# Two constants made on other engines, one table load first, and a planner told when engines begin

## The chip, the cores and the metric

The kernel runs on one core of one Trainium2 chip. The core has a matrix engine (PE, with a queue of weight loads, PEld), a vector engine (DVE), a scalar engine with function tables (ACT), Pool and SyncE (SP), which here only starts transfers. All engines run their own instruction queue in order and meet through semaphores. The metric is the device time of one execution in microseconds (us), and a time is the median over several runs.

## The reference

Linear attention without a softmax is followed by a two-layer network with softplus. The bridge between them turns (batch, head, row, feature) into 4608 tokens of 512 features.

```python
kv  = einsum('bhsd,bhse->bhde', k, v)          # 8 batches, 8 heads, 576 rows, 64 features
o   = einsum('bhsd,bhde->bhse', q, kv)
o   = o / sqrt(mean(o*o, -1) + 1e-6) * g_norm  # g_norm: 64 numbers
x   = o, heads beside each other               # 4608 x 512
h   = x @ w_in                                 # 512 x 2048
g   = maximum(h, 0) + log1p(exp(-abs(h)))
out = g @ w_out                                # 2048 x 512
```

The inputs q, k, v and g_norm are 32-bit floats. The two weight matrices come in 64-bit floats, and the kernel reads each value as two 32-bit words.

## The kernel before

**Precision by parts.** PE multiplies in a reduced 32-bit format (fp32r), so each operand of the two large products is split into a high part and two low ones. A step of the first product (`mm1`, L668) is 12 matmuls of 384 columns: 3 parts by 4 blocks of 128 features. A step of the second (`mm2`, L675) is 3 groups of 3 matmuls of 512 columns. 16 chunks of 128 hidden features times 12 blocks of 384 tokens make 192 steps, in three phases of chunks, with the partial output written to memory between phases.

**Weights.** Each of 32 pieces (16 chunks of w_in, 16 of w_out, 128 x 512 values) is loaded in 512 KB of raw words (`fetch`, L275) into one of two buffers `raw`. Then ACT makes a square from the upper words (`square`, L286), DVE builds the 32-bit value (`high1` L290, `high2` L294, `mask` L299, which reads ACT's square, `power` L307, `rest` L312, `total` L316), and ACT sums what is beyond range (L303). A raw buffer is free again after `rest`. `divide` makes the three parts: ACT the high part (L348), DVE the remainder (L351), ACT the second part (L355). For the first four chunks the third part comes from PE: two matmuls, one with the identity (L366) and one with the negative identity `minus_r` (L367), whose sum ACT scales (L370).

**Attention.** For each batch, `kv_of` loads k and v (L491, L493, the last 64 rows as `tail` in L483 and L485) and multiplies them on PE (L505 for batches 0 and 1, L513 otherwise and for the tails), and ACT copies the result to `kv_diag` (L520, L521). `rows` does 128 tokens: q is turned (PE L585 and ACT L592 for the first two batches, DVE L560 later), multiplied with kv (L530), squared on ACT (L598), summed on DVE (L535), raised to the power -0.5 on Pool (L538, L539), scaled on DVE (L542), and turned on PE (L547). `split` makes the three parts of x^T with g_norm as a factor by partition: ACT the high part with `g_down` (L437), which is g_norm times a number just under 1, DVE the others with `g_col` (L440, L444). ACT copies x^T for later phases (L607), and SP stores it (L608).

**Order.** Nothing is scheduled by the framework. The kernel adds tasks with an estimated duration, dependencies, buffers and a place in the order (`pos`) to a `Plan`. `Plan.order` (L67) plays the tasks through on five engines and one transfer server: it keeps a date at which each engine and the transfers are free, takes the task that can begin first (among those within `SOON` = 150 ns on one engine, the lowest `pos`), and gives it its buffers. The dates are only used for the order in which each engine gets its instructions; on the chip everything runs as its waits allow. A transfer may be issued when its server will be free within 2500 ns, and lands 2000 ns after its own share of the server. While PE has nothing planned before the first `mm1`, the plan puts filler matmuls of the identity in (`warm`, L784), from `BEGIN` = 4000 ns on, as many of 400 ns as fit before the next real task.

**The preamble.** Before the planned tasks, L747 to L758 issue by hand: two small loads of g_norm into `g_col` from ACT's queue (L748), `g_down` on ACT (L749), the table of softplus for ACT (L750), the identity on Pool (by a helper), its fp32r copy on DVE (L753), `minus_r` on ACT (L754), and memsets on DVE (L755 to L758). The table that holds softplus also serves ACT's other functions in this kernel: after L750 the trace has no other table load.

Of the kernel before, what the change touches and what calls it, by code (L numbers as in the profile page):

```python
# [13 lines left out]
ALU = mybir.AluOpType  # L14
# [8 lines left out]
DOWN_G = 1.0 - 0.99 * 2.0 ** -13  # L23
# [17 lines left out]
class Plan:  # L41
# [2 lines left out]


    HANDOVER = {"PE": 250, "ACT": 120, "DVE": 120, "POOL": 150, "SP": 0}
    BEGIN = 4000
    SOON = 150

# [17 lines left out]
    def order(self):  # L67
        waiting = {id(t): len(t.after) + (t.follows is not None) for t in self.tasks}
        users = {}
        for t in self.tasks:  # L70
            for a in t.after + ([t.follows] if t.follows else []):
                users.setdefault(id(a), []).append(t)
        ready = {}
        for t in self.tasks:
            if not waiting[id(t)]:
                t.ready = 0
                ready.setdefault(t.engine, []).append(t)
        free = {r: [(0, i) for i in range(n)] for r, n in self.rings.items()}
        engine_free = {"PE": 0, "ACT": 0, "DVE": 0, "POOL": 0, "SP": 0}
        dma_free = 0  # L80
        last_read = {}
        done, left = [], len(self.tasks)
        while left:
            best = None
            for engine, tasks in ready.items():
                options = []
                for t in tasks:
                    at = max(engine_free[engine], t.ready)
                    if t.size:
                        at = max(at, dma_free - 2500)  # L90
                    for i, s in enumerate(t.take):
                        others = sum(u.ring == s.ring for u in t.take[:i])
                        if len(free[s.ring]) <= others:
                            break
                        at = max(at, sorted(free[s.ring])[others][0])
                    else:
                        options.append((at, t))
                if not options:
                    continue
                first = min(at for at, _ in options)  # L100
                at, t = min(((at, t) for at, t in options if at <= first + self.SOON),
                            key=lambda o: (o[1].pos, o[0]))
                if engine == "PE" and self.spare and self.spare[-1].start is None:
                    ring, run, ns, _ = self.spare
                    begin = max(engine_free["PE"], self.BEGIN, min(free[ring])[0] if free[ring] else at)
                    if begin + ns <= at:
                        s = Slot(ring)
                        at, t = begin, Task("PE", ns, lambda s=s: run(s), [], 0.0, [s], [s], 0)
                        s.readers = 1
                if best is None or at < best[0]:  # L110
                    best = (at, t)
            if best is None:
                raise RuntimeError("the plan is stuck at " + str([(e, t.pos, [s.ring for s in t.take if not free[s.ring]]) for e, ts in ready.items() for t in ts][:20]))
            at, t = best
            if t in ready[t.engine]:
                ready[t.engine].remove(t)
                left -= 1
            for s in t.take:
                place = min(free[s.ring])
                free[s.ring].remove(place)  # L120
                s.place = place[1]
            t.start = at
            engine_free[t.engine] = at + t.ns
            t.end = at + t.ns + self.HANDOVER[t.engine]
            if t.size:
                dma_free = max(dma_free, at + t.ns) + t.size
                t.end = dma_free + 2000
            for s in t.give:
                s.readers -= 1
                last_read[id(s)] = max(last_read.get(id(s), 0), t.end)  # L130
                if not s.readers:
                    free[s.ring].append((last_read[id(s)], s.place))
            for u in users.get(id(t), ()):
                waiting[id(u)] -= 1
                if not waiting[id(u)]:
                    u.ready = max([a.end for a in u.after] + ([u.follows.start] if u.follows else []), default=0)
                    ready.setdefault(u.engine, []).append(u)
            done.append(t)
        return sorted(done, key=lambda t: t.start)
# [3 lines left out]
def kernel(  # L143
# [24 lines left out]
    nc = tc.nc  # L168
# [31 lines left out]
    ident = ident_r.bitcast(F32)  # L200
    minus_r = const.tile([P, P], F32R, name="minus_r")
    g_col = const.tile([P, 1], F32, name="g_col")
    g_down = const.tile([P, 1], F32, name="g_down")
# [542 lines left out]

    for e in range(2):  # L747
        nc.scalar.dma_start(out=g_col[e * D:(e + 1) * D], in_=g_norm.rearrange("(d one) -> d one", one=1))  # L748
    nc.scalar.mul(g_down, g_col, DOWN_G)  # L749
    nc.scalar.preload_act_table_set("softplus")  # L750
    scratch = kv_diag[0][:, 0]
    make_identity(nc, scratch)
    nc.vector.tensor_copy(ident_r, scratch)  # L753
    nc.scalar.mul(minus_r, ident, -1.0)  # L754
    nc.vector.memset(half, -0.5)  # L755
    nc.vector.memset(big, 2.0 ** 30)
    for x in kv_diag + tails:
# [62 lines left out]
```

## Time and profile before

| | |
|---|---|
| median of 6 runs | 918.31 us (917.41 to 919.20) |
| the profiled execution | 919.17 us |
| its span, first to last instruction | 917.4 us |
| mean granted PE clock | 0.992 |
| PE busy | 897.9 us (98%) |
| DVE, ACT, Pool busy | 626.6, 414.7, 80.3 us |
| read from and written to memory | 91.75 and 38.80 MB |
| first `mm1` matmul (L668) | 43.21 us |
| last stretch of matmuls | 909.09 to 913.47 us |

Times within a profile are microseconds from the start of its span. A line of the timeline names the start, the length, the engine, the line of the kernel, the operation, the tile written and the tile read, shapes and count; in brackets stands how long the engine stood idle before it, and what ended that. SPq and ACTq are the parts of SP and ACT that start transfers. In a table of stretches each row has the length, then the busy time of PE, PEld, DVE, ACT and Pool with instruction counts, then the granted PE clock (1.00 is full), the DMA engines' busy share and their GB/s. Busy shares of DMA can exceed 1, since packets overlap.

### The profile page before, as it was taken

The numbers are of one execution on the slowest core, as the hardware profiler recorded it, in microseconds if no ns is written. First come the engines' busy times: TensorE is split into PE (matmuls) and PEld (weight loads), VectorE is DVE, ScalarE is ACT, GpSimd is POOL, SyncE is SP. The second block draws the span as 40 slices with busy tenths as digits, with TensorE's granted clock in tenths as the row PEclk, the third lists the DMA queues.
The fourth block names the chain that finished last, engine by engine and source line by source line (L and its number), as shares of the span: only waits on it lengthen the run. The fifth ranks groups of instructions, "written<-read, shape, count | busy, mean of one in ns | idle before, by whom it ended". The sixth has DMA issues, their size and how long they took to land.

```text
span 917.4 us, 13377 instructions
## 1 busy us (share of the span) xinstructions
PE 897.9 (98%) x4863; PEld 812.7 (89%) x4863; DVE 626.6 (68%) x1055; ACT 414.7 (45%) x799; POOL 80.3 (9%) x78
## 2 busy tenths in 40 slices
PE   5899999999999999999999999999999999999998
PEld 4689899989998999999999999999999999998987
DVE  5877887876458887789756778888444455555553
ACT  4766555444334656455434455446323333333331
POOL 0314421311122100000000000000000000000000
PEclk7999999999999999999999999999999999999999
DMA  8999999397783654445434444643321433333323
GB/s 225 260 215 240 235 207 203 89 219 145 176 140 106 150 150 127 126 139 172 150 104 127 150 126 139 204 148 120 104 68 35 138 103 101 108 104 104 104 69 104
DMA packets 230386, 131.44 MB, mean 143 GB/s; under 512 B 127408, under 2 KB 204208, under 8 KB 230320
## 3 DMA queue, kind: packets, MB, share of 16 engines
q1 hardware_dynamic: 230160, 130.59, 53.8%
q8 instruction: 38, 0.62, 0.3%
q14 instruction: 28, 0.23, 0.1%
q10 hardware_dynamic: 160, 0.00, 0.0%
HBM read 91.75 MB, written 38.80 MB: 142 GB/s over the span
## 4 chain that ended last, share of the span: by engine, by line
PE 95%; DVE 1%; ACT 1%; DMA 1%; POOL 1%; issue 0%; ACTq 0%
PE s L675 44%; PE h L668 43%; PE o L530 3%; PE o L513 3%; DMA g_col<-in_g_norm_dram 1%; DMA m<-in_v_dram 1%; PE tp L547 1%; POOL r L539 0%; DVE xv L440 0%; ACT m L607 0%; PE o L505 0%; PE h L367 0%; DVE m L294 0%; DVE xv L444 0%; PE tp L585 0%
## 5 line engine op out<-in xcount | busy, mean ns | idle before, releaser
L668 PE MATMUL h<-xv,w 128*128 128x384 f32 x2304 | 434.3, 337 | 0.0
L675 PE MATMUL s<-w,gv 128*128 128x512 f32 x1728 | 434.2, 395 | 0.0
L668 PEld LDWEIGHTS h<-xv,w 128*128 128x128 f32 x2304 | 406.6, 188 | 14.9 <-ACT m L607 0.2
L675 PEld LDWEIGHTS s<-w,gv 128*128 128x128 f32 x1728 | 319.4, 188 | 58.9 <-issue 0.5
L688 ACT ACTIVATE g<-h 128x384 f32<-128x384 f32 x192 | 94.3, 491 | 395.2 <-PE h L668 390.7
L679 DVE TENSOR_TENSOR gv<-g,gv 128x384 fp32r<-128x384 f32 x192 | 106.5, 555 | 180.0 <-ACT gv L690 179.2
L690 ACT ACTIVATE gv<-g 128x384 fp32r<-128x384 f32 x192 | 100.8, 525 | 23.4 <-PE s L675 16.0
L683 DVE SCALAR_TENSOR_TENSOR gv<-gv 128x384 fp32r<-128x384 f32 x192 | 106.9, 557 | 6.1
L440 DVE SCALAR_TENSOR_TENSOR xv<-m,g_col,xv 128x512 fp32r<-128x512 f32 x102 | 75.9, 744 | 1.3 <-ACT xv L437 1.3
L444 DVE SCALAR_TENSOR_TENSOR xv<-xv 128x512 fp32r<-128x512 f32 x108 | 74.4, 689 | 2.6
L437 ACT ACTIVATE xv<-m,g_down 128x512 fp32r<-128x512 f32 x102 | 69.4, 710 | 0.8 <-DMA m<-x 0.8
L539 POOL TENSOR_TENSOR r<-r,half 128x8 f32<-128x8 f32 x36 | 64.8, 1800 | 3.0
L715 DVE SCALAR_TENSOR_TENSOR m<-s,scale,m 128x512 f32<-128x512 f32 x24 | 17.9, 747 | 30.1 <-PE s L675 30.1
L530 PE MATMUL o<-kv_diag,m 128*128 128x128 f32 (+1 forms) x296 | 36.9, 276 | 0.0
L530 PEld LDWEIGHTS o<-kv_diag,m 128*128 128x128 f32 (+1 forms) x296 | 35.1, 179 | 1.9 <-issue 1.0
L538 POOL TENSOR_SCALAR r<-r 128x8 f32<-128x8 f32 x36 | 14.8, 412 | 241.7 <-DVE r L535 241.4
L715 DVE SCALAR_TENSOR_TENSOR m<-s,m 128x512 f32<-128x512 f32 x36 | 23.8, 685 | 13.5 <-PE s L675 13.4
L535 DVE TENSOR_REDUCE r<-x 128x8 f32<-128x512 f32 x36 | 24.5, 681 | 10.7 <-ACT x L598 10.7
L542 DVE TENSOR_TENSOR x<-o,r 128x512 f32<-128x512 f32 x33 | 22.7, 686 | 12.6 <-POOL r L539 12.6
L303 ACT ACTIVATE sq<-sq,big 128x512 bf16<-128x512 bf16 x32 | 22.9, 715 | 10.2 <-DVE m L299 10.2
L299 DVE SCALAR_TENSOR_TENSOR m<-sq,m 128x512 f32<-128x512 bf16 x32 | 22.1, 690 | 6.3 <-ACT sq L286 4.9
L355 ACT ACTIVATE w<-m 128x512 fp32r<-128x512 f32 x32 | 20.1, 627 | 13.9 <-DVE m L351 13.7
(69 smaller groups left out, 454.5 us busy)
## 6 DMA issues: line engine op xcount, KB each, us to landing
m<-x SPq DMA_DIRECT2D x102, 256.0 KB, 4.7
part<-m SPq DMA_DIRECT2D x72, 256.0 KB, 2.8
m<-part SPq DMA_DIRECT2D x72, 256.0 KB, 3.7
raw<-in_moe_w_in_dram SPq DMA_DIRECT2D x16, 512.0 KB, 5.3
m<-in_v_dram SPq DMA_DIRECT2D x32, 256.0 KB, 4.0
raw<-in_moe_w_out_dram SPq DMA_DIRECT2D x16, 512.0 KB, 5.3
qa<-in_q_dram SPq DMA_DIRECT2D x24, 288.0 KB, 6.4
m<-in_k_dram SPq DMA_DIRECT2D x48, 128.0 KB, 3.7
```

Of the source, the lines that this page charges most:

```text
L437: nc.scalar.activation(cols(0, F32R), x.tile, func=AF.Identity, scale=g_down)
L440: nc.vector.scalar_tensor_tensor(out=cols(1, F32R), in0=x.tile, scalar=g_col, in1=cols(0), op0=ALU.mult, op1=ALU.subtract)
L444: nc.vector.scalar_tensor_tensor(out=cols(2, F32R), in0=cols(1), scalar=-RADIX, in1=cols(0), op0=ALU.mult, op1=ALU.add)
L530: nc.tensor.matmul(y[r0:r0 + n, p::NP], lhsT=qT.tile[:, p, r0:r0 + n], rhs=kv_diag[b % 2][:, p].rearrange("r (h d) -> r h d", d=D), start= ...
L539: nc.gpsimd.tensor_tensor(out=r.tile, in0=r.tile, in1=half, op=ALU.pow)
L668: nc.tensor.matmul(hp, lhsT=w_in.tile[:, i, kd * P:(kd + 1) * P], rhs=xv.tile[:, i, kd], start=(m == 0), stop=(m == 3 * KD - 1))
L675: nc.tensor.matmul(mine[i].tile, lhsT=gv.tile[:, m, i * P:(i + 1) * P], rhs=w_out.tile[:, m], start=(c == cs[0] and m == 0), stop=(c == cs ...
L679: nc.vector.tensor_tensor(out=gv.tile[:, 1], in0=g.tile, in1=gv.tile.bitcast(F32)[:, 0], op=ALU.subtract)
L683: nc.vector.scalar_tensor_tensor(out=gv.tile[:, 2], in0=f32[:, 1], scalar=-RADIX, in1=f32[:, 0], op0=ALU.mult, op1=ALU.add)
L688: a = add("ACT", 490, lambda: nc.scalar.activation(new(g, [P, NT]), h.tile, func=AF.Softplus, scale=1.0 + E), [a], s, [g], [h])
L690: a = add("ACT", 530, lambda: nc.scalar.activation(new(gv, [P, 3, NT], F32R)[:, 0], g.tile, func=AF.Copy, scale=DOWN), [a], s, [gv])
L715: a = add("DVE", 700, lambda: nc.vector.scalar_tensor_tensor(out=new(ot, [P, d_model]), in0=bank.tile, scalar=(scale if ph == LAST else 1. ...
```

## The change

Three things are changed. `g_down` is made by Pool with a tensor_scalar, behind the identity, where ACT made it ahead of its table; so the first thing on ACT behind its two small loads is the load of softplus's table. `minus_r` is made by DVE with a tensor_scalar right after the identity's copy, where ACT made it. The planner starts with engine dates of 2500 (PE, ACT, Pool), 4000 (DVE) and 700 ns (SP) and a transfer date of 1500 ns instead of zeros.

```diff
     HANDOVER = {"PE": 250, "ACT": 120, "DVE": 120, "POOL": 150, "SP": 0}
+    READY = {"PE": 2500, "ACT": 2500, "DVE": 4000, "POOL": 2500, "SP": 700}
     BEGIN = 4000
     SOON = 150
...
         free = {r: [(0, i) for i in range(n)] for r, n in self.rings.items()}
-        engine_free = {"PE": 0, "ACT": 0, "DVE": 0, "POOL": 0, "SP": 0}
-        dma_free = 0
+        engine_free = dict(self.READY)
+        dma_free = 1500
         last_read = {}
...
     for e in range(2):
         nc.scalar.dma_start(out=g_col[e * D:(e + 1) * D], in_=g_norm.rearrange("(d one) -> d one", one=1))
-    nc.scalar.mul(g_down, g_col, DOWN_G)
     nc.scalar.preload_act_table_set("softplus")
     scratch = kv_diag[0][:, 0]
     make_identity(nc, scratch)
     nc.vector.tensor_copy(ident_r, scratch)
-    nc.scalar.mul(minus_r, ident, -1.0)
+    nc.vector.tensor_scalar(out=minus_r, in0=ident, scalar1=-1.0, scalar2=None, op0=ALU.mult)
+    nc.gpsimd.tensor_scalar(out=g_down, in0=g_col, scalar1=DOWN_G, scalar2=None, op0=ALU.mult)
     nc.vector.memset(half, -0.5)
     nc.vector.memset(big, 2.0 ** 30)
     for x in kv_diag + tails:
```

## The prediction

> **What bounds the kernel now.** I read the page's head first: busy time by engine.
>
> ```profile
> PE 897.9 (98%) x4863; PEld 812.7 (89%) x4863; DVE 626.6 (68%) x1055; ACT 414.7 (45%) x799; POOL 80.3 (9%) x78
> PEclk7999999999999999999999999999999999999999
> ```
>
> PE is busy for all but 19.5 us of the 917.4 us span. The table of stretches says where those 19.5 us lie.
>
> ```profile
> 0.00:56.00 56.00, 40.42 (x321) 32.40 (x322) 40.27 (x72) 34.58 (x67) 11.87 (x16) 0.88 0.90 241
> 56.00:300.00 244.00, 244.00 (x1456) 224.95 (x1455) 177.82 (x299) 118.92 (x230) 62.34 (x56) 1.00 0.82 176
> 300.00:917.40 617.40, 613.47 (x3091) 555.39 (x3089) 408.52 (x686) 261.25 (x502) 6.09 (x6) 1.00 0.40 121
> ```
>
> The second number is PE's busy time: 15.6 us are lost before 56 us, none from 56 to 300, 3.9 after. PE's waits end with the one at 53.3 us. So the end is set by how early PE becomes full, plus a fixed sum of matmuls, and a change in the preamble is worth what it moves that moment. Part of the early busy time is also no work: the 21 filler matmuls of L784 take 3.75 + 0.80 + 1.23 + 0.71 + 0.47 + 1.60 = 8.56 us by the timeline. Next, the first 15 us of the timeline:
>
> ```profile
> 0.72 1.19 ACTq L748 DMA_DIRECT2D g_col<-in_g_norm_dram  x2
> 1.32 0.23 DVE L753 CAST ident_r<-kv_diag 128x128 fp32r<-128x128 f32 x1 [1.32 <-POOL kv_diag masks.py:199]
> 1.60 3.75 PE L784 MATMUL h<-ident_r 128*128 128x512 f32 x9 [1.60 <-DVE ident_r L753]
> ...
> 6.49 0.69 DVE L294 SCALAR_TENSOR_TENSOR m<-raw,m 128x512 uint32<-128x512 uint32 x1
> ...
> 7.91 1.28 ACT L749 ACT_TABLE_LOAD   x1 [7.91 <-DMA g_col<-in_g_norm_dram]
> 9.21 0.20 ACT L749 ACTIVATE g_down<-g_col 128x1 f32<-128x1 f32 x1
> ...
> 9.43 1.28 ACT L750 ACT_TABLE_LOAD   x1
> 10.72 0.31 ACT L754 ACTIVATE minus_r<-ident_r 128x128 fp32r<-128x128 f32 x1
> ...
> 10.94 0.65 ACT L286 ACTIVATE sq<-raw 128x512 bf16<-128x512 bf16 x1
> 11.61 0.69 DVE L299 SCALAR_TENSOR_TENSOR m<-sq,m 128x512 f32<-128x512 bf16 x1 [4.43 <-ACT sq L286]
> ...
> 13.58 0.34 SPq L275 DMA_DIRECT2D raw<-in_moe_w_out_dram  x1
> ```
>
> ACT does nothing until the 64 numbers of g_norm have landed at 7.9 us: they arrive behind the large loads. Then come a table load, g_down, a second table load and minus_r, and only at 10.94 us the square of the first weight, whose raw words DVE began to work on at 6.02. DVE stands for 4.43 us (7.18 to 11.61). SP stands too: the third raw load needs the buffer that DVE's L312 (12.80 to 13.49) gives back, and everything behind it in SP's queue (tails, q, batch 1) waits with it. The DMA share by the microsecond shows the hole:
>
> ```profile
> 12.00:13.00 1.00, 0.00 (x0) 0.00 (x0) 0.93 (x3) 0.66 (x2) 0.00 (x0) 0.50 0.57 186
> 13.00:14.00 1.00, 0.00 (x0) 0.00 (x0) 0.97 (x2) 0.83 (x3) 0.00 (x0) 0.50 0.01 2
> 14.00:15.00 1.00, 0.06 (x1) 0.06 (x1) 0.97 (x3) 0.63 (x1) 0.00 (x0) 0.50 0.48 94
> ```
>
> The last two numbers are DMA share and GB/s; before them stands PE's granted clock. The chain of waits agrees: its early part is the 6.55 us of DMA for g_col, then ACT L749, L750, L754, L286, then DVE.
>
> **The change part by part.**
>
> *g_down to Pool.* ACT loses the wait to 7.91, one table load (1.28) and the 0.20 us activation. Pool gains one 128x1 tensor_scalar behind the identity's instructions (done at 1.3 us). Pool's 128x8 ones (L538) take 0.24 to 0.61 us, so it ends near 8.5 us. Behind it in Pool's queue is the first L538, at 27.45; the first reader of g_down is ACT's L437 at 32.65. Cost nothing, with 19 us of cover; without that cover it would cost its 0.6.
>
> *minus_r to DVE.* ACT loses 0.31 us. DVE gains about 0.23 us (L753 on the same shape took 0.227), ahead of its memsets, which then end at 4.2 instead of 3.98; the raw words come at 6.02. Cost nothing; without that idle time 0.23. It is read at 16.61 by PE.
>
> *Table first.* ACT's queue is now two DMA issues (to 1.91), one load (to about 3.2), square. The load has 2.8 us of cover before 6.02. The trace starts the next activation 0.01 us after a load. The Trainium skill (ScalarE: Activation LUTs, section on what ACT_TABLE_LOAD costs) charges a drain of about 1.38 us besides, 2.66 in all; by that the load would end near 4.6, still before the raw words, and the sum would not change.
>
> *Together.* The square can start at 6.02 (DVE's L290 starts on the same landing) and ends at 6.67. DVE's L299 is then held only by L294, so it starts at 7.20 for 11.61: 4.41 us earlier. L312 ends at 9.08, SP issues the third raw load about 9.1 for 13.58. From 11.61 on DVE is 7.4, 8.7, 8.2 and 8.3 us busy in the four ten-microsecond stretches to 50, so it and SP lead the preamble, and both move 4.41.
>
> *What is late next: DMA.* At 9.1 us loads are still running at a share of 1.1 until 12.5, so the loads that move up queue behind them. The share leaves 0.43 + 0.99 + 0.52 + 0.15 = 2.1 us unused from 12 to 16, 0.6 more to 20, little from 20 to 31, and 2.4 more to 49 (0.47, 0.44 and 0.42 of it in 46 to 49). Landings can thus be 2.7 us earlier in the twenties and over 4.4 by 49. Batch 1's first k and v have no slack (used at 27.67, as they land) and may be up to 4.41 - 2.7 = 1.7 late. Behind them PE queues L530 and L585, whose copy L592 has 0.5 us of slack on ACT. So between 0 and 1.7 us is lost; I take 0.5, nearer to nothing, because only the first batch-1 matmuls are used as they land. After 56 us PE never waits, and SP's waits are on compute engines, which move along.
>
> *The planner's new dates.* They set only the order of instructions. The first load's planned landing moves from 4250 to (1500 + 1800 + 2000) = 5300, and from the third load on SP follows the DMA date, also +1050. All compute tasks but a memset follow landings, so all dates move by 1050 together and the order stays; Pool, ACT and DVE begin before 5300. One date is fixed, BEGIN = 4000: the first stretch of fillers runs to 8800 instead of 7750, which makes 12 for 9. Three more at 0.417 us end at 6.6 us, against the first real matmul at 9.32, held by DMA: they cost nothing, and 1.25 us if that landing were early.
>
> *The clock.* It falls to 0.50 2.6 us after the fillers end at 5.35 and returns at 21.5, some 4 us into the first unbroken run (from 17.33). L367 takes 0.80 us in it and 0.39 later; 32 L505 take 1.91 on the chain, and 16 later take 0.69. With the fillers to 6.6 PE's gap is 2.7 instead of 3.97 us. Kept at full, the chain's 16.6 to 21.7 would save up to 0.4 + 0.7 + 0.4 + 0.8 = 2.3 us (L367, L505, L784, L513), of which DVE, nearly full there, lets perhaps 1.2 through. If the first run after the shift is broken by a DMA wait, the low clock lasts longer instead. I take 0, the same stretch moved along. The Trainium skill (TensorE: Matmul & The Clock Gate, Part 1) has the clock fall only after an idle window of about 3.4 us; by that the new gap would not trip it and the sum would be 1.2 us better, but this trace dropped it after 2.6.
>
> *Sum.* 4.41 - 0.5 = 3.9 us. The profiled execution took 919.17 (span 917.40, 1.77 around it) and would become 915.3; the median of the runs is 0.86 below the profiled one, so 918.31 - 3.9 = 914.4.
>
> **The rivals.**
>
> *A, forecast:* 3.9, with 2.7 (the whole 1.7 lost) to 4.9 (the square's own 10.94 to 6.03, if ACT led): 913.4 to 915.6.
>
> *B, transfers set the pace throughout:* only the hole of 2.1 us is won: 916.2. For it: shares near 1.0 from 20 to 45. Against: PE's DMA waits after 12 us total 0.2 before the last one of 1.3 at 53.3.
>
> *C, the clock stays up:* 1.2 more than A: 913.2, or down to 912.0 with all of the 2.3.
>
> *D, no gain:* what ends the preamble is elsewhere, the landing of v at 53.17 or Pool's chain of L539 (1.67 to 2.08 us each). 918.3. Against: all of these are issued or fed by queues that move.
>
> *E, slower, by the clock:* the loads of the tails come late, PE's run at 17.33 breaks into pieces, and the clock stays at 0.50 past 21.5. PE is about three quarters busy from there to 43, so each microsecond at half clock costs about 0.5 net of idle. It eats the 3.9 at 8 us more of low clock and shows as slower (1.8 beyond) from 11.4; all the way to 43 it costs 11 - 3.9 = 7: 925. Against: the shifted run has the same matmuls behind it.
>
> **How the numbers follow.** A measurement of this kernel tells about 0.2% (1.84 us) from no change. A 0.62, B 0.14, C 0.07, D 0.09, E 0.08. A, B and C are faster by over 0.2%: 0.83; D is the same: 0.09; E slower: 0.08. The predicted time is A's. The range 912.8 to 917.1 holds A, B with a microsecond either way at 916.2, and half of C; it leaves out D, E and the rest of C, 0.2.
>
> **What would show it.** Right: one table load, before 4 us; no wait of DVE for the square; L299 near 7.2; the third raw load near 9.1; DMA without a hole at 13; the first L668 (43.21 now) near 39.3 and PE's last wait near 49; every stage from there on earlier by the same amount. Twelve fillers at the start. Wrong, if: PE waits on m from DMA after 20 us take more than 2 us; the clock is 0.50 past 21.5; the instruction order differs beyond the fillers and the moved lines; or a wait of PE appears after 56.

## The result and the profile after

The kernel after takes 916.71 us (914.97 to 917.90, 17 runs) against 918.34 us (917.29 to 921.35, 35 runs) for the kernel before, run beside it. The ratio is 0.9978, with a 95% interval of 0.9972 to 0.9985: 2.0 us less, between 1.4 and 2.6 (the two medians as they stand differ by 1.6). The prediction said 914.4, in a range of 912.8 to 917.1.

Line numbers in the kernel after are one higher than before from L268 on: the square is L287, the mask L300, `mm1` L669. First the head of its page, the busy time by engine.

```profile
PE 899.3 (98%) x4866; PEld 813.9 (89%) x4866; DVE 626.9 (68%) x1056; ACT 413.1 (45%) x796; POOL 80.9 (9%) x79
```

Three matmuls more (the fillers), three ACT instructions fewer and one more each on DVE and Pool: the change did what its diff says. The table of stretches (length, busy time of PE, PEld, DVE, ACT and Pool, clock, DMA share, GB/s):

```profile
0.00:56.00 56.00, 43.55 (x336) 35.06 (x336) 41.85 (x74) 33.99 (x67) 12.36 (x17) 0.91 0.97 249
56.00:300.00 244.00, 244.00 (x1455) 225.08 (x1454) 178.25 (x300) 119.15 (x232) 62.48 (x56) 1.00 0.83 174
300.00:915.70 615.70, 611.76 (x3079) 553.71 (x3077) 406.84 (x683) 259.96 (x500) 6.06 (x6) 1.00 0.40 122
```

PE's lost time before 56 us fell from 15.6 to 12.4 us, of which 1.17 is the longer first row of fillers (4.92 for 3.75). From 56 us on PE loses as little as before: nothing until 300, 3.9 us after. The first `mm2` matmul starts at 52.49 us for 54.19, and what follows it lasts 863.2 us in both profiles (917.4 and 915.7 less these). Of the kernel before, then of the kernel after:

```profile
54.19 1.64 PE L675 MATMUL s<-w,gv 128*128 128x512 f32 x6
...
52.49 1.64 PE L676 MATMUL s<-w,gv 128*128 128x512 f32 x6
```

The DMA share of the first 56 us rose from 0.90 to 0.97, and the hole at 13 us is gone: 314 GB/s move from 13 to 14 us where 2 did. The timeline shows the stall gone and what took its place.

```profile
1.58 0.23 DVE L754 TENSOR_SCALAR minus_r<-ident_r 128x128 fp32r<-128x128 f32 x1
...
1.60 4.92 PE L785 MATMUL h<-ident_r 128*128 128x512 f32 x12 [1.60 <-DVE ident_r L753]
...
1.94 1.28 ACT L750 ACT_TABLE_LOAD   x1 [1.94 <-issue]
...
5.44 0.68 ACT L287 ACTIVATE sq<-raw 128x512 bf16<-128x512 bf16 x1 [2.22 <-DMA raw<-in_moe_w_in_dram]
...
6.72 0.69 DVE L300 SCALAR_TENSOR_TENSOR m<-sq,m 128x512 f32<-128x512 bf16 x1
...
8.17 0.52 POOL L755 TENSOR_SCALAR g_down<-g_col 128x1 f32<-128x1 f32 x1 [6.88 <-DMA g_col<-in_g_norm_dram]
...
9.04 0.38 SPq L276 DMA_DIRECT2D raw<-in_moe_w_out_dram  x1
...
17.13 0.43 DVE L291 TENSOR_SCALAR m<-raw 128x512 uint32<-128x512 uint32 x1 [1.85 <-DMA raw<-in_moe_w_out_dram]
...
18.48 1.40 PE L514 MATMUL o<-tail,tail 128*128 128x128 f32 x8 [2.36 <-DMA tail<-in_v_dram]
...
23.11 0.67 ACT L287 ACTIVATE sq<-raw 128x512 bf16<-128x512 bf16 x1
...
23.82 0.69 DVE L300 SCALAR_TENSOR_TENSOR m<-sq,m 128x512 f32<-128x512 bf16 x1 [1.71 <-ACT sq L287]
```

One table load at 1.94; the square at 5.44, as the raw words land; DVE's mask at 6.72 without a wait, 4.89 us earlier; the third raw load issued at 9.04, 4.54 us earlier. Up to here all is as predicted, but for the raw words, which land 0.6 us sooner. Then come new waits: DVE 1.85 us for the third raw piece, PE 2.36 us for the tail of v. The chain of waits (start, length, what) of the kernel after has both its early transfers in it:

```profile
3.75 7.24 DMA m<-in_v_dram
...
11.00 7.34 DMA tail<-in_v_dram
...
18.48 1.40 PE o L514 x8
```

The list of issues gives the time from issue to landing (the last number, in us). Of the kernel before:

```profile
raw<-in_moe_w_out_dram SPq DMA_DIRECT2D x1, 512.0 KB, 3.4
tail<-in_v_dram SPq DMA_DIRECT2D x1, 128.0 KB, 3.1
```

and of the kernel after:

```profile
raw<-in_moe_w_out_dram SPq DMA_DIRECT2D x1, 512.0 KB, 8.1
tail<-in_k_dram SPq DMA_DIRECT2D x2, 64.0 KB, 7.7
tail<-in_v_dram SPq DMA_DIRECT2D x1, 128.0 KB, 7.3
```

Issued 4.5 us earlier, the third raw piece lands at 17.1 us where it landed at 17.0 before. Two stretches of the kernel after, in the columns of the table above, say more:

```profile
9.00:12.00 3.00, 2.00 (x32) 1.88 (x32) 2.93 (x6) 1.57 (x3) 0.00 (x0) 0.50 1.11 357
14.00:17.00 3.00, 2.11 (x27) 1.51 (x23) 0.69 (x1) 0.55 (x2) 0.00 (x0) 0.70 1.15 142
```

From 9 to 12 us, while the last of batch 0's k and v are on their way, 357 GB/s move at a share of 1.11. From 14 to 17 us the raw piece, the tails and q are in flight together; the share is even higher, but only 142 GB/s move. Meanwhile DVE works 0.69 of 3 us and ACT 0.55.

Where the 4.5 us went can be followed step by step:

| event | before | after | earlier by |
|---|---|---|---|
| mask of the first weight (L299, L300) | 11.61 | 6.72 | 4.89 |
| third raw load issued | 13.58 | 9.04 | 4.54 |
| DVE begins on that piece (L290, L291) | 19.77 | 17.13 | 2.64 |
| PE begins on the tails (L513, L514) | 19.84 | 18.48 | 1.36 |
| mask of the fourth weight | 25.25 | 23.82 | 1.43 |
| first `mm1` | 43.21 | 41.78 | 1.43 |
| first `mm2` | 54.19 | 52.49 | 1.70 |

PE takes the tails 1.36 us earlier; behind them in its queue are the two matmuls with the identities (L367, L368), on these waits ACT's L371 (20.77 for 22.21), behind that in ACT's queue stands the fourth weight's square (23.11 for 24.55), and on that waits DVE's mask. So the lateness of one landing goes from PE to ACT to DVE, and the 1.43 stays to the first `mm1`.

### The profile page after: what moved, and what is told of

Read it like the earlier page. It is cut to its first block, busy times and chain, and to the rows that moved or that the text cites. A ratio compares the mean times of both kernels' runs of the same rounds, so it can differ in the third digit from the quotient of the medians.

```text
span 915.7 us, 13383 instructions
## 1 busy us (share of the span) xinstructions
PE 899.3 (98%) x4866; PEld 813.9 (89%) x4866; DVE 626.9 (68%) x1056; ACT 413.1 (45%) x796; POOL 80.9 (9%) x79
## 4 chain that ended last, share of the span: by engine, by line
PE 95%; DMA 2%; DVE 1%; SPq 1%; POOL 1%; issue 0%; ACT 0%
PE s L676 44%; PE h L669 44%; PE o L531 3%; PE o L514 3%; DMA m<-in_v_dram 1%; DMA tail<-in_v_dram 1%; PE tp L548 1%; POOL r L540 0%; SPq L494 0%; DVE xv L441 0%; PE tp L586 0%; DVE xv L445 0%; PE h L367 0%; PE h L368 0%; DVE r L536 0%
## 5 line engine op out<-in xcount | busy, mean ns | idle before, releaser
L669 PE MATMUL h<-xv,w 128*128 128x384 f32 x2304 | 434.3, 337 | 0.0
L669 PEld LDWEIGHTS h<-xv,w 128*128 128x128 f32 x2304 | 406.6, 188 | 14.9 <-issue 0.2
L531 PE MATMUL o<-kv_diag,m 128*128 128x128 f32 (+1 forms) x296 | 36.9, 276 | 0.0
L531 PEld LDWEIGHTS o<-kv_diag,m 128*128 128x128 f32 (+1 forms) x296 | 35.1, 179 | 1.9 <-issue 1.0
L287 ACT ACTIVATE sq<-raw 128x512 bf16<-128x512 bf16 x32 | 21.2, 662 | 15.5 <-DMA raw<-in_moe_w_in_dram 11.6
```

Source lines behind the costliest of these rows:

```text
L531: nc.tensor.matmul(y[r0:r0 + n, p::NP], lhsT=qT.tile[:, p, r0:r0 + n], rhs=kv_diag[b % 2][:, p].rearrange("r (h d) -> r h d", d=D), start= ...
L669: nc.tensor.matmul(hp, lhsT=w_in.tile[:, i, kd * P:(kd + 1) * P], rhs=xv.tile[:, i, kd], start=(m == 0), stop=(m == 3 * KD - 1))
```

## The experiments

The theory after the result: the stall is worth its 4.4 us, and what is missing was taken by the early transfers, which take longer when they move up. Its rivals: the planner's new dates changed the order; the clock took it; only some of the edits count; one load, not the transfers as a whole, is late. Ratios are against the kernel before, run on the same chip.

**The dates alone.**

```diff
+    READY = {"PE": 2500, "ACT": 2500, "DVE": 4000, "POOL": 2500, "SP": 700}
...
-        engine_free = {"PE": 0, "ACT": 0, "DVE": 0, "POOL": 0, "SP": 0}
-        dma_free = 0
+        engine_free = dict(self.READY)
+        dma_free = 1500
```

> The kernel before with the planner's new dates alone. Theory T (the order is the same and the gain comes from the constants): only three more fillers at the start, time within 0.2% of before, 918.3. Rival P (part of the gain is the planner's): faster by some 0.5 to 2 us.

918.40 us, ratio 1.0001 (0.9993 to 1.0010). The stall stands as it was, 4.58 us until L300 at 11.54. The dates alone are worth nothing that can be measured.

**The constants and the table alone** (the kernel after with the planner's old zeros).

```diff
-        engine_free = dict(self.READY)
-        dma_free = 1500
+        engine_free = {"PE": 0, "ACT": 0, "DVE": 0, "POOL": 0, "SP": 0}
+        dma_free = 0
```

> The changed kernel with the planner's old dates (zeros). Theory T: the whole gain stays, about 2.0 us under before (ratio 0.9978), nine fillers at the start. Rival P: the gain shrinks by what the dates brought, to 0.5 to 1.5 us.

916.18 us, ratio 0.9976 (0.9967 to 0.9985): the whole gain without the dates. The first `mm1` came at 41.93 and the span was 915.4 (41.78 and 915.7 after). The table of stretches gives a granted clock of 1.00 throughout for this profile, but the matmuls themselves say otherwise:

```profile
9.93 1.12 PE L506 MATMUL o<-m,m 128*64 128x64 f32 x16 [4.11 <-DMA m<-in_v_dram]
...
26.44 0.69 PE L506 MATMUL o<-m,m 128*64 128x64 f32 x16
```

The same 16 matmuls took 1.12 us at a clock of 0.50 in the profile after, and 0.69 at 1.00. The trace's records of the clock begin only at 21.2 us in this run, and where there is none the table shows 1.00. So PE ran at the low clock from 9.9 to some 21 us here too, and this run does not tell what the low clock costs; the run with the tails first and the fillers does (below).

**`minus_r` left on ACT.**

```diff
-    nc.vector.tensor_scalar(out=minus_r, in0=ident, scalar1=-1.0, scalar2=None, op0=ALU.mult)
+    nc.scalar.mul(minus_r, ident, -1.0)
```

> The changed kernel with minus_r made by ACT again, behind the table load. Theory: ACT is done with it near 3.6 us, ahead of the raw words, so the time is the changed kernel's, 916.3 to 916.7: the whole gain is g_down's wait and table load. Rival: moving minus_r is worth its 0.3 us.

916.55 us, ratio 0.9983 (0.9973 to 0.9992), the kernel after within the interval. ACT makes it at 3.23 us, 0.01 us after the end of its table load and before the raw words, and the square still starts at 5.43. What counts is that nothing on ACT waits for g_norm ahead of the square. The move of `minus_r` to DVE adds nothing.

**Larger packets, in both kernels.** The tails and q rows move as 2 KB rows; the bytes read and the count of them stay, but other rows of k, v and q are read.

```diff
+                    flat = src[b].rearrange("h s d -> (h s d)")[:n * H * D].rearrange("(p f) -> p f", p=n)
+                    if b < 2:
+                        nc.sync.dma_start(out=s.tile[:n].rearrange("p h d -> p (h d)"), in_=flat)
+                        return
...
-                for e in range(2):
-                    nc.sync.dma_start(out=natural(q_s, at_qa)[:n, e::2], in_=halves(q[b, :, s0:s0 + n], e))
+                flat = q[b].rearrange("h s d -> (h s d)")[:n * H * D].rearrange("(p f) -> p f", p=n)
+                nc.sync.dma_start(out=natural(q_s, at_qa)[:n].rearrange("p h d -> p (h d)"), in_=flat)
```

> The kernel before, with the q rows and the 64-row tails of k and v of batches 0 and 1 read from memory as whole rows of 2 KB (the same bytes into the same tiles, in an eighth of the packets). The values are then those of other rows, so the output is not the reference's; the work is the same. Theory T (DMA time goes by packets, and the preamble is short of it): the preamble gets shorter also here, by 1 to 4 us, but DVE's stall of 4.4 us before the first mask stays. Rival B (DMA time goes by bytes): no change, 918.3. It is the base for the next run.

> The changed kernel with the same 2 KB rows. Theory T (the 4.5 us that the third raw load is issued earlier were eaten because it shared the DMA engines with the 256-byte packets of the tails and of q): this load now lands 3 to 5 us after its issue at 9.0, near 13 to 14 instead of 17.1, DVE does not wait for it, and the change is worth 3.5 to 4.4 us against the run with 2 KB rows and the old constants. Rival C (the low PE clock and the order of ACT ate the rest): the change is worth 2 us here as well.

Before with it: 917.82 us, 0.9989 (0.9980 to 0.9997). After with it: 916.46 us, 0.9978 (0.9970 to 0.9987). The change is worth 917.82 - 916.46 = 1.36 us here (1.0 by the ratios), no more than without. The landings stay late; the issues of the kernel after with large packets, and its stretch from 14 to 16 us:

```profile
raw<-in_moe_w_out_dram SPq DMA_DIRECT2D x1, 512.0 KB, 7.6
...
tail<-in_v_dram SPq DMA_DIRECT2D x1, 128.0 KB, 8.1
```

```profile
14.00:16.00 2.00, 1.92 (x25) 1.29 (x21) 0.69 (x1) 0.59 (x1) 0.00 (x0) 0.50 1.03 165
```

165 GB/s at a share of 1.03: the theory that the small packets of tails and q slow the raw load fell. Later the large packets do go faster (from 20 to 22 us 364 GB/s at a share of 1.10, against 230 at 1.29 after), but the time is the same.

**The raw load alone.** In the kernel after, the tails and everything behind them in SP's queue are held until the third raw piece has landed, by one number that Pool copies from it into the tail's buffer.

```diff
+                    if b == 0 and s is ks:
+                        nc.gpsimd.tensor_copy(s.tile[:1, 0, :1], raw_slots[1].tile[:1, 0, 0:1].bitcast(F32))
```

> The changed kernel, with the batch-0 tails, and so all loads behind them on SP, held until the third raw load has landed (Pool copies one number of it into the tail tile, which the tail load then overwrites). Theory O (the third raw load, the tails and q slow each other down when they are in flight together, 7 to 8 us each for 3.1 to 3.4 one after the other): the raw load lands by 15.0 instead of 17.1, the tails, issued only then, about 3.5 us later at 18 to 18.5, as now; time within 0.7 us of the changed kernel's. Rival S (14 to 18 us is a slow stretch whatever is in flight): the raw load lands after 16.5 also alone, the tails after 20, and the time is 1 to 2 us over the changed kernel's.

919.98 us, ratio 1.0024 (1.0016 to 1.0033): slower than the kernel before, which neither theory expected. Its stretches:

```profile
9.00:12.00 3.00, 1.82 (x33) 1.63 (x34) 2.93 (x6) 1.63 (x3) 0.00 (x0) 0.84 1.10 353
12.00:14.00 2.00, 2.00 (x22) 1.35 (x24) 1.39 (x2) 1.40 (x4) 0.00 (x0) 0.50 0.84 309
14.00:16.00 2.00, 1.22 (x19) 0.83 (x16) 1.70 (x3) 1.15 (x3) 0.35 (x1) 0.89 0.02 8
```

Two things follow. Issued at 8.78 and with nothing behind it, the raw piece lands at 14.96, 6.2 us after its issue, where it took 8.1 beside the tails and q; but that is still not the 3.4 of the kernel before, since the k and v issued ahead of it come first: the last of them lands at 13.7. So even alone a load that is issued 4.8 us earlier lands only 2.0 us earlier than before (16.98). And the idle hole behind it (8 GB/s from 14 to 16 us) costs more than the raw piece gains: the tails are issued at 15.45 to 16.9, PE takes them at 19.82, and the fourth raw piece keeps DVE waiting 4.60 us, until 23.47.

**The tails ahead of the raw piece** in SP's queue.

```diff
-    for t in plan.order():
+    tasks = plan.order()
+    late = next(t for t in tasks if t.engine == "SP" and t.pos == FETCH[1])
+    tail = next(t for t in tasks if t.engine == "SP" and any(u.ring == "tail1" for u in t.take))
+    tasks.remove(late)
+    tasks.insert(tasks.index(tail) + 1, late)
+    for t in tasks:
         t.run()
```

> The changed kernel, with the third raw load moved behind the batch-0 tails in SP's order, nothing else moved. Theory N (what is left of the preamble hangs on the landing of the tails, 18.3 us): tails issued from 8.9 us land by 16.5, PE's L514 starts 2 us or more earlier, the first mm1 too, and the time falls to 914 to 915.5. Rival D (DVE's wait for the third raw load decides): the raw load lands at 17 or later, and the time is the changed kernel's or up to 1 us worse.

916.77 us, ratio 0.9986 (0.9978 to 0.9995), no better than after. From PE's timeline:

```profile
16.69 1.13 PE L514 MATMUL o<-tail,tail 128*128 128x128 f32 x8 [0.51 <-DMA tail<-in_v_dram]
...
31.78 0.69 PE L506 MATMUL o<-m,m 128*64 128x64 f32 x16 [0.91 <-DMA m<-in_v_dram]
...
35.85 0.69 PE L506 MATMUL o<-m,m 128*64 128x64 f32 x16 [2.09 <-DMA m<-in_v_dram]
...
42.62 2.36 PE L669 MATMUL h<-xv,w 128*128 128x384 f32 x12
```

PE takes the tails 1.8 us earlier than after, and then waits 3.0 us for batch 1's v, for which it did not wait after. The first `mm1` is even later, 42.62 for 41.78. So it is not one load that is late: take one away from the chain, and the next has its place. (Behind this wait the clock also falls, from 38.0 to 41.4 us.)

**More fillers against the low clock**, 7 more matmuls in the first row and 5 more in the row where PE waits for the tails.

```diff
+        fillers.append(s)
+        extra = {1: 7, 13: 5}.get(len(fillers), 0)
+        y = new(s, [P, 4, P])
+        for _ in range(1 + extra):
...
```

> The changed kernel with 7 more fillers in the first stretch and 5 more at 15.5 us, where PE is idle for 3.1 and 2.4 us. Theory C (part of the missing gain is the low PE clock, 0.50 from 9 to 15.6 and from 19.4 to 22.7): the clock stays at 1.00 from 9.6 or at least past 18.5, L514 to the first L531 gets 1 to 1.8 us shorter, and the time falls by 0.8 to 1.8 us. Rival T (transfers decide alone): within 0.4 us of the changed kernel.

916.33 us, ratio 0.9985 (0.9977 to 0.9994). The clock still fell, at 11.4 us, but was back at 18.3 (after it was at 0.50 from 8.9 to 15.8 and from 19.2 to 22.6). PE's L531 came at 21.48 for 22.64, but then PE waits 0.59 us for batch 1's v at 31.76 and 1.32 at 35.39, and the clock falls once more, from 35.3 to 38.7. No gain that can be measured.

**Both together**, the tails first and the fillers.

```diff
+    late = next(t for t in tasks if t.engine == "SP" and t.pos == FETCH[1])
...
+        extra = {1: 7, 13: 5}.get(len(fillers), 0)
...
```

> The changed kernel with both edits that made its early stages earlier: the tails ahead of the third raw load, and the 12 more fillers. Theory B: L514 and the first L531 come earlier than in either, but PE then waits for k and v of batch 1 and the first second-product matmul stays between 51.2 and 52.5; time within 0.7 us of the changed kernel's. Rival: the two add up, and it is 1.5 us or more under the changed kernel.

916.70 us, ratio 0.9988 (0.9979 to 0.9997). The first `mm1` came a little earlier (41.36), with a wait of 1.39 us for batch 1's v at 35.61. The two don't add up. This is the one profile whose preamble ran at the full clock: its records say 1.00 from 7.3 us on, and the matmuls agree.

```profile
9.99 0.69 PE L506 MATMUL o<-m,m 128*64 128x64 f32 x16 [0.85 <-DMA m<-in_v_dram]
...
12.10 0.50 PE L367 MATMUL h<-w,ident_r 128*128 128x512 f32 x1
```

After, these took 1.12 and 0.80 us. So a preamble without the low clock, and with the tails first, is not measurably faster than the kernel after.

**Fewer early transfers, in both kernels.** Left out are the tails of batches 0 and 1 and the q rows of the first four token tiles, 1.5 MB (Pool fills that buffer instead).

```diff
+                    if b < 2:
+                        return
...
+                    if at_qa:
+                        nc.gpsimd.memset(q_s.tile, 0.0)
+                if at_qa:
+                    return
```

> The kernel before without 1.5 MB of its early loads: the tails of k and v of batches 0 and 1 and the q rows of the first four token tiles are not loaded (those tiles hold zeros), so the output is not the reference's; all engines do the same work but for one memset on Pool. It is the base for the next run. Theory B (the transfers pace the preamble as a whole): the first second-product matmul (54.2 us) comes 1 to 4 us earlier. Rival: engines pace it with ACT's late start, and it moves less than 1 us.

> The changed kernel without the same loads. Theory B: with the transfers relieved the change is worth what ACT's earlier start gives, 3 to 4.4 us against the run before (914 or less), and the third raw load lands by 15.2. Rival E (what is not won is lost on the engines, by the clock or ACT's order): 2 us or less against the run before, as with all loads.

Before with it: 917.14 us, ratio 0.9991 (0.9982 to 1.0000). After with it: 912.67 us, ratio 0.9942 (0.9929 to 0.9955; 5 runs). From the timeline of the first, then of the second:

```profile
11.20 0.69 DVE L299 SCALAR_TENSOR_TENSOR m<-sq,m 128x512 f32<-128x512 bf16 x1 [4.43 <-ACT sq L286]
...
52.60 1.64 PE L681 MATMUL s<-w,gv 128*128 128x512 f32 x6
```

```profile
6.72 0.69 DVE L300 SCALAR_TENSOR_TENSOR m<-sq,m 128x512 f32<-128x512 bf16 x1
...
8.68 0.34 SPq L276 DMA_DIRECT2D raw<-in_moe_w_out_dram  x1
...
15.41 0.42 DVE L291 TENSOR_SCALAR m<-raw 128x512 uint32<-128x512 uint32 x1
15.47 1.73 PE L516 MATMUL o<-tail,tail 128*128 128x128 f32 x8
...
48.06 1.64 PE L682 MATMUL s<-w,gv 128*128 128x512 f32 x6
```

DVE's new wait for the raw piece is gone (it lands at 14.8), and PE goes through the tails at 15.47. The mask comes 4.48 us earlier than in the kernel before with the same loads left out, and the first `mm2` 4.54 us earlier: the head start arrives whole. The change is worth 917.14 - 912.67 = 4.47 us here (by the spans 915.8 - 911.2 = 4.6); with the two intervals together that is some 3.0 to 5.9, above the 2.0 of the whole kernels. By the ratios, the same 1.5 MB cost the kernel before 1.0000 - 0.9991 = 0.0009 of its time, 0.8 us, and the kernel after 0.9978 - 0.9942 = 0.0036, 3.3 us. So with the transfers lightened the change brings the 4.41 us that the stall was priced at, and what is missing otherwise, 2.4 us, is the early transfers' doing. The edit takes the loads, SP's time to issue them and PE's waits for them away together, so it doesn't say which of these weighs most. Pool's filling of the buffer takes 2.02 us, from 1.24 us on in the first of the two and from 7.91 in the second, and the DVE instruction beside it takes longer (the identity's copy 2.02 us for 0.23, L291 0.97 for 0.42); in the first that delay is over before DVE's stall, which is as long as ever (4.43).

## Why the prediction was right in sign and too large in size

**What held.** "Table first", "g_down to Pool" and "minus_r to DVE" went as written: one table load, ended by 3.22 us, DVE's tensor_scalar of 0.23 us, Pool's of 0.52, both beside other work. The drain of about 1.38 us that the prediction weighed is not seen: with `minus_r` left on ACT the next activation starts at 3.23. "Together" gave 4.41 us and 9.1 us for the raw load's issue; the runs show 4.89, because the raw words landed at 5.44 and not 6.02, and 9.04. That the head start is worth its 4.41 if nothing eats it is shown by the pair with fewer transfers (4.47, between some 3.0 and 5.9). "The planner's new dates" held: 12 fillers for 9, otherwise the same order on every engine, and nothing gained or lost by the dates alone. That the preamble sets the end held too: 863.2 us from the first `mm2` on in both, and no wait of PE after 56.

**What failed** is the term "What is late next: DMA". It took 0.5 us, within 0 and 1.7. Measured is 4.41 - 2.0 = 2.4 us, beyond its upper end. Three things were wrong in that step. It held only batch 1's first k and v to have no slack, because in the profile before only they are used as they land. But the tails had little more: they landed 1.3 us before their use (15.39 + 3.1 = 18.5, used at 19.84), and the third raw piece 2.8 us before its own (16.98, 19.77), in the kernel before:

```profile
19.77 0.42 DVE L290 TENSOR_SCALAR m<-raw 128x512 uint32<-128x512 uint32 x1
...
19.84 1.88 PE L513 MATMUL o<-tail,tail 128*128 128x128 f32 x8
```

If the use would move up by 4.4 and the landing can't, only that slack is won: PE's tails came 1.36 us earlier and DVE's work on the raw piece 2.64. The first piece of batch 1, on which the term hung, is not waited for in the profile after (26.29 for 27.67). Secondly, it took the share that DMA leaves unused as room into which loads can move. The share was at 1.10 until 12 us, and a load issued at 9 us stands behind k and v whatever the hole at 13 looks like: alone, it won 2.0 us of its 4.8. Thirdly, it let the loads keep their rate when they move up; they landed 7 to 8 us after issue for 3, at 142 GB/s.

**Rival B** (the transfers set the pace throughout, only the hole of 2.1 us is won, 916.2) comes nearest, and its cause, the transfers, is the one that the pair with fewer of them bears out; that it is the hole itself that was won, no run shows. The time of 916.71 lies in the stated range only because that range was drawn to hold B as well (the forecast's own went to 915.6): the forecast itself, 914.4, is 2.3 us off, more than half of the gain it named. The prediction held against it that PE's waits for DMA after 12 us total 0.2. That was no argument: these waits were hidden behind DVE's stall of 4.43 us, and 2.36 and 1.85 us of them appear as soon as it is gone. Slack in a profile with a stall is slack with that stall in it. The order of the tails and the raw piece, the fillers and the packet size each moved waits and no time that can be measured, as B would have it.

**The clock** was taken at nothing, and no run shows that it cost anything. In the profile after it fell at 8.9 us, 2.4 us after the fillers' end at 6.52, was back at 15.8, and was at 0.50 again from 19.2 to 22.6, behind PE's wait for the tails. That is past 21.5, the sign that rival E named, but not at E's cost. The profiles of the kernel after and of its variants hold very different stretches of low clock before 30 us: 10.2 us after, 13.7 with `minus_r` on ACT and with the large packets, none from 7.3 us on with the tails first and the fillers. Their times are 916.71, 916.55, 916.46 and 916.70. And the pair with fewer transfers brought 4.47 us with the clock at 0.50 from 10.1 to 16.9 in the second. The Trainium skill (TensorE: Matmul & The Clock Gate, Part 1), which the prediction weighed, has the clock fall after an idle window of about 3.4 us; this profile shows the fall after 2.4. In the trace's records the early stretches of one clock last 3.41 us or a multiple of it (6.83, 10.24, 13.65), and the one that ends with the fall (5.54 to 8.95) still holds the last 0.98 us of the fillers. So a gap somewhat under 3.4 us is no safety, and no step of a forecast should hang on it.

**The signs.** Of the marks named, the first `mm1` was to come near 39.3 (41.78) and PE's last wait was to end near 49 (51.60). Both missed by some 2.5 us, by the term above. The sum of 4.41 - 0.5 = 3.9 becomes 4.41 - 2.4 = 2.0.

## What to carry to other kernels

When a stall is removed, list the loads that its end releases and, for each load needed in the next microseconds, the slack between landing and use; the head start is lost as far as it exceeds that slack, unless the landings move too, and a load that moves into a stretch where the transfers are already full does not land earlier by what it is issued earlier. That no engine waits for DMA in a profile says nothing about DMA once the stall that hid it is gone. To learn what a change of the order is worth apart from the transfers, run it and its base with some of the early loads left out: here that pair showed 4.47 us where the whole kernel showed 2.0.

## What the runs showed of the hardware

The busy share of the DMA engines did not tell the rate: 357 GB/s at 1.11, 142 GB/s at 1.15, 165 GB/s at 1.03 with larger packets. The Trainium skill (DMA: Bandwidth & Descriptors, Specifications) gives about 358 GB/s as the limit of what memory delivers to one core. The 350 and 357 GB/s of 9 to 12 us in the profiles before and after lie close to that, but from 8 to 9 us the same profiles moved 381 and 384, so it is no sharp ceiling here, and it does not explain the 142. Why the raw piece, tails and q together run at less than half the rate stays open. Larger packets did not cure it, and without the tails and q behind it the raw piece took 6.2 us for 8.1. Other queues for the tails were not tried.

The granted clock of a profile can be missing: in the runs of the constants alone and of the lightened kernel before, the records begin at 21.2 and 22.5 us and the tables show 1.00 ahead of that, while 16 matmuls of the first batch take 1.12 us instead of 0.69. The length of a known group of matmuls tells.

A load's issue can itself take long. In the profile after SP spends 3.27 us on the issue of the fourth raw load, in the profile before 0.37 us:

```profile
13.32 3.27 SPq L276 DMA_DIRECT2D raw<-in_moe_w_in_dram  x1
```

With the early loads left out the same issue took 0.37 us at 13.39. What SP waits for there the trace doesn't say.
